# Routing tokens in groups of 10, 10, 5, 5, 3, 2 and 1 tiles, with rank products over shifted columns and one epsilon addition per tile

## The chip, the core and the metric

The kernel runs on one core of one Trainium2 chip. The metric is the device time of one execution in microseconds (us). A core has a matrix engine (TensorE, PE in the rows, with its weight loads shown apart as PEld), VectorE (DVE), ScalarE (ACT), GpSimd (POOL) and SyncE (SP), which issues most DMAs. Each engine works through its own instructions in the order in which they were written, and waits on semaphores for the others.

## The reference

The program chains three parts: pooled attention, a mixture of experts with one expert per token, and a dense feed-forward part.

```python
k_p = k.reshape(B, H, Sp, 8, D).mean(axis=3)      # B, H, S, D = 8, 8, 576, 64; Sp = 72
v_p = v.reshape(B, H, Sp, 8, D).mean(axis=3)
scores = scale * q @ k_p^T
attn = exp(scores - max);  attn = attn / (attn.sum(-1) + 1e-09);  out = attn @ v_p
x = out.transpose(0, 2, 1, 3).reshape(4608, 512)
logits = x @ w_gate + modality_bias[modality_id]  # 8 experts
e_idx = argmax(logits);  gate_w = softmax(logits)[e_idx]
y[token] = gate_w * (relu(x[token] @ w1[e_idx]) @ w2[e_idx])      # 512 -> 1024 -> 512
h = y @ w_in;  result = (h * clip(h + 3, 0, 6) / 6) @ w_out       # 512 -> 2048 -> 512
```

## The kernel before, in words

**Attention** is the first 190 us or so of the program. The 4608 tokens are 36 tiles of 128. The loop at L567 takes one round per tile, for tiles 0 to 32; tiles 33 to 35 follow it, written out. A round works on three tiles at once, so that each tile's work is spread over several rounds:

- `stage_t` (L302) transposes the five blocks of tile i's exponentials on PE into `tps` (L307, this opens the round) and copies them on ACT to `eT` (L309).
- `stage_e` takes the exponentials of tile i + 2 on ACT (L299, L300).
- `stage_x` (L346) multiplies the heads 4 to 7 of tile i - 1 by `rs`, in four ACT instructions (L349), out of the second half of that tile's `ups`.
- `stage_q` transposes the queries of tile i + 4 on PE (L252) and copies them on ACT (L254).
- In some rounds keys and values of a later batch follow (`prep`, `prep2`): PE products `kvps` (L179) and `pw` (L224), ACT copies `vT` (L197), DVE copies `bd` (L188), POOL products `vb` (L231). Pooling of keys and values is DVE's (L173).
- `stage_s` makes the scores of tile i + 3 on PE (`sps`, L281), then on DVE the maxima `mx` (L283) and the differences `d` (L286 or L289).
- `stage_a` (L319) multiplies `eT` of tile i by `vb` on PE into `ups` (L328), in two halves z = 0 and 1 of four heads each, three matmuls a half (twice that for a tile that spans two batches). Each half has a buffer of its own, `u0` and `u1`, in PSUM. DVE then adds the epsilon to each half's sums (L336, two instructions), takes the reciprocal `rs` (L338) and multiplies the heads 0 to 3 (L341). `xo` hands the second half to the next round's `stage_x`.

**Routing.** `ups` carries the gate logits of each head beside its output, so that a row of `xg` holds what the routing of its token needs. Tiles are routed in the groups of `GROUPS`: six of 5 tiles, then 3, 2 and 1. When the last tile of a group is behind, `route` (L361) writes 11 DVE operations on the whole group (and one exponential on ACT) into the list `fill`; `run_fill` (L356) puts one operation of this list behind each DVE operation of `stage_s` and `stage_a`. The first of them (L381) sums the logits over the heads; `oh` (L387) is the one-hot choice of expert.

When all 11 are written, `route_b` (L399) counts on PE how many tokens in front chose the same expert (`rps`, L406): for tile r of n, r matmuls with `ones` and one with the triangle `tri`, and n for the sum over the group. `route_c` (L411) adds five DVE operations (L425 to L429), the last of which casts the row numbers `ix` (L419), and POOL then scatters a tile's rows to DRAM by an indirect DMA (L435), from round `SC0` = 13 two a round. Behind group `FE` = 4 (tiles 20 to 24) `first_expert` (L695) puts 12 small DVE operations in a second list. In round `XL` = 28 what is left in both lists is issued, the scatters that are due are written, and `first_x` (L854) loads the rows of the first expert (`cxg`, by SP at L858) and its weights (`ws`).

**The experts** start in the tail of attention: POOL multiplies the loaded rows by their gate (L829), PE transposes them (`x0`, L837, into `xps`). The two feed-forward parts fill the rest of the program; the change touches nothing there.

The places to follow are `ups` in `stage_a`, `stage_x`, `run_fill`, and the loop's order of calls: `stage_t`, `stage_e`, `stage_x`, `route`, `stage_q`, `prep`s, `stage_s`, `route_b`, `stage_a`, scatters.

Of the kernel before, what the change touches and what calls it, by code (L numbers as in the profile page):

```python
# [8 lines left out]
F32 = mybir.dt.float32  # L9
F32R = mybir.dt.float32r  # L10
BF16 = mybir.dt.bfloat16
# [3 lines left out]
ALU = mybir.AluOpType  # L15
# [4 lines left out]
P = 128  # L20
B, H, S, D = 8, 8, 576, 64
POOL = 8
# [4 lines left out]
E = 8  # L27
# [5 lines left out]
XE = D + E  # L33
GC = H * XE
XW = GC + 2
UX = XE + 1
# [6 lines left out]
REST = (3, 11, 4, 12, 5, 13, 6, 14, 7, 15)  # L43
ORDER = (0, 4, 1, 5, 3, 2, 6)
KR = (0, 160, 288, 448)
GROUPS = ((0, 5), (5, 5), (10, 5), (15, 5), (20, 5), (25, 5), (30, 3), (33, 2), (35, 1))
SC0 = 13
FE = 4
XL = 28
WU = 10  # L50
WS = (-1, -1, 6, 7)
# [22 lines left out]
def attention(tc, g, moe, ins, xr_d):  # L74
    nc = tc.nc
    q, k, v, mid, w_gate, mbias = ins
    es, es_q, es_kv, es_p = ExitStack(), ExitStack(), ExitStack(), ExitStack()
    pool = lambda n, b, st=es, **kw: st.enter_context(tc.tile_pool(name=n, bufs=b, **kw))
    c1 = pool("ac", 1)
    p2 = pool("ap2", 2)  # L80
    p3 = pool("ap3", 3)
    xp = pool("axp", 4)
    rp = pool("arp", 3)
    qp = pool("aq", 3, es_q)
    kvp = pool("akv", 2, es_kv)
# [1 line left out]
    ps_t = pool("ps_t", 1, es_p, space=PSUM)  # L87
    ps_u = pool("ps_u", 1, es_p, space=PSUM)
    ps_q = pool("ps_q", 1, es_p, space=PSUM)

    tiles = []
    for pr in range(B // 2):
# [2 lines left out]
    NTI = len(tiles)  # L95
# [29 lines left out]
    tri = c1.tile([P, P], BF16, name="tri")  # L125
    nc.gpsimd.memset(tri, 1.0)
    nc.gpsimd.affine_select(tri, tri, pattern=[[1, P]], compare_op=ALU.is_gt, fill=0.0, base=0, channel_multiplier=-1)
    ones = c1.tile([P, P], BF16, name="ones")
    nc.gpsimd.memset(ones, 1.0)
    tok = c1.tile([P, NTI], F32, name="tok")  # L130
    t9 = tok.rearrange("p (r t) -> p r t", t=9)
    for c0, n, b0, cm, p0, p1 in ((0, 4, 0, 4, 0, P), (4, 2, S, 4, 0, P), (7, 2, S + 2, 4, 0, P), (6, 1, 512, 1, 0, 64), (6, 1, S + 512, 1, 64, P)):
# [179 lines left out]
    xg = {}  # L312
# [6 lines left out]
    def stage_a(i):  # L319
        o = ETt.pop(i)  # L320
        if i == NTI - 2:
            u = [ps_s.tile([P, 512], F32, name="ups", tag="s")[:, 0:4 * UX].rearrange("p (j x) -> p j x", x=UX) for z in range(2)]
        else:
            u = [ps_u.tile([P, 4, UX], F32, name="ups", tag=f"u{z}") for z in range(2)]
        for z in range(2):
            for n, (c, j, h) in enumerate(((2 * z, 4 * z, 0), (2 * z + 1, 4 * z + 2, 2), (4, 8 + 2 * z, 1))):
                for b, p0, p1 in halves(i):
                    nc.tensor.matmul(u[z][p0:p1, h:h + 2].rearrange("p j x -> p (j x)"), o[:, c, p0:p1],  # L328
                                     vb[b % 3][:, j:j + 2].rearrange("p j x -> p (j x)"), start=n == 0, stop=n == 2)
        j, r, n = group_of(i)  # L330
        if r == 0:
            xg[j] = xp.tile([P, n, XW], F32, name="xg", tag="xg")
        x = xg[j][:, r, 0:GC].rearrange("p (h x) -> p h x", x=XE)
        rs = p3.tile([P, H], F32, name="rs", tag="rs")
        for z in range(2):
            nc.vector.tensor_scalar(rs[:, 4 * z:4 * z + 4], u[z][:, :, XE], POOL * 1e-9, None, op0=ALU.add)  # L336
            run_fill()
        nc.vector.reciprocal(rs, rs)  # L338
        run_fill()
        xo.append((x, u[1], rs))  # L340
        nc.vector.tensor_tensor(x[:, 0:4], u[0][:, :, 0:XE], rs[:, 0:4].unsqueeze(2).to_broadcast([P, 4, XE]), op=ALU.mult)  # L341
        run_fill()
# [8 lines left out]
    fill, fill2 = [], []  # L351
# [4 lines left out]
    def run_fill():  # L356
        for _ in range(rate[0]):
            if fill or fill2:
                (fill or fill2).pop(0)()

    def route(j):  # L361
        i0, n = GROUPS[j]
        x = xg[j]
        sh = [P, n, E]
        v = nc.vector
        t = lambda nm, s_, dt=F32: rp.tile(s_, dt, name=nm, tag=nm)
        l, ex, w, oh = t("l", sh), t("ex", sh), t("w", sh), t("oh", sh, BF16)
        m, m2 = t("m", [P, n, 1]), t("m2", [P, n, 1])

        gs = t("gs", [P, n, 1])  # L370

        def shift():
            v.tensor_tensor(l, l, m.to_broadcast(sh), op=ALU.subtract)
            nc.scalar.activation(ex, l, AF.Exp)

        def last():
            v.reciprocal(x[:, :, GC:GC + 1], gs)
            rt[j] = (x, oh)

        crit = [  # L380
            lambda: v.tensor_reduce(l, x[:, :, 0:GC].rearrange("p n (h x) -> p n x h", x=XE)[:, :, D:XE], AX.X, ALU.add),  # L381
            lambda: v.tensor_tensor(l, l, bia[:, i0:i0 + n], op=ALU.add),
            lambda: v.tensor_reduce(m, l, AX.X, ALU.max),
            shift,
            lambda: v.scalar_tensor_tensor(w, l, 0.0, rev8.unsqueeze(1).to_broadcast(sh), op0=ALU.is_equal, op1=ALU.mult),
            lambda: v.tensor_reduce(m2, w, AX.X, ALU.max),
            lambda: v.tensor_tensor(oh, w, m2.to_broadcast(sh), op=ALU.is_equal),  # L387
        ]
        rest = [
            lambda: v.tensor_copy(x[:, :, GC + 1], tok[:, i0:i0 + n]),  # L390
            lambda: v.tensor_reduce(gs, ex, AX.X, ALU.add),
            lambda: v.tensor_scalar(gs, gs, 1e-9, None, op0=ALU.add),
            last,
        ]
        if j >= len(GROUPS) - 3:
            return crit[:5] + rest[:1] + crit[5:6] + rest[1:2] + crit[6:] + rest[2:]
        return crit + rest

    def route_b(new=lambda: ps_s.tile([P, 512], F32, name="rps", tag="s")):  # L399
        ops = []  # L400
        for j, (x, oh) in list(rt.items()):
            i0, n = GROUPS[j]
            ps = new()
            for r in range(n + 1):
                for r2 in range(min(r + 1, n)):
                    nc.tensor.matmul(ps[:, r * E:(r + 1) * E], tri if r2 == r else ones, oh[:, r2], start=(r2 == 0),  # L406
                                     stop=(r2 == min(r, n - 1)))
            ops += route_c(j, ps, *rt.pop(j))
        return ops

    def route_c(j, ps, x, oh):  # L411
        i0, n = GROUPS[j]
        sh = [P, n, E]
# [95 lines left out]
    ps = kv_ps()  # L509
# [57 lines left out]
    for i in range(NTI - 3):  # L567
        if i == 25:
            es_kv.close()
            moe.open1()  # L570
        if i == NTI - 4:
            es_q.close()
            moe.open2()
        if i == XL:
            each(fill)
            each(fill2)
            del fill[:], fill2[:]
            put_rows()
            tc.add_to_no_dep_group("scatter", moe.first_x())
        stage_t(i)  # L580
        stage_e(i + 2)
        if xo:
            stage_x()
        for j, (a, n) in enumerate(GROUPS):
            if a + n == i:
                fill.extend(route(j))
        if i > 0 and i + 4 < NTI:
            stage_q(i + 4)
        for fn_ in sched.get(i, ()):
            fn_()  # L590
        stage_s(i + 3)
        if i == NTI - 4:
            sp(-1)
        for fn_ in sched2.get(i, ()):
            fn_()
        fill.extend(route_b())
        stage_a(i)
        if i == 0:
            prep_k(1)
            stage_q(4)  # L600
        for _ in range(2):
            if pend and i >= SC0:
                scatter(*pend.pop(0))
    i = NTI - 3
# [41 lines left out]
    ps = unit_table(tc, g, moe.ps)  # L646
# [649 lines left out]
```

## Time and profile before

| what | value |
|---|---|
| median of 3 runs | 1426.13 us (1425.29 to 1426.59) |
| the profiled execution's own time | 1420.61 us |
| its span in the trace | 1418.9 us |
| PE busy over the span | 1371.0 us (97%) |
| DVE, ACT, POOL busy | 940.7, 624.1, 156.5 us (66%, 44%, 11%) |
| loop over tiles 0 to 32, first to last `tps` | 25.3 to 187.9 us |

The profiled execution is 5.5 us below the median of the other runs, so a difference that is worked out from the trace is set against 1420.61 us and then carried over to the median. "Busy" leaves out waits; the busy shares are means over stages that differ. The times of the rows count from the start of the span.

### The profile page before, as it was taken

The numbers are of one execution on the slowest core, as the hardware profiler recorded it, in microseconds if no ns is written. First come the engines' busy times: TensorE is split into PE (matmuls) and PEld (weight loads), VectorE is DVE, ScalarE is ACT, GpSimd is POOL, SyncE is SP. The second block draws the span as 40 slices with busy tenths as digits, with TensorE's granted clock in tenths as the row PEclk, the third lists the DMA queues.
The fourth block names the chain that finished last, engine by engine and source line by source line (L and its number), as shares of the span: only waits on it lengthen the run. The fifth ranks groups of instructions, "written<-read, shape, count | busy, mean of one in ns | idle before, by whom it ended". The sixth has DMA issues, their size and how long they took to land.

```text
span 1418.9 us, 24229 instructions
## 1 busy us (share of the span) xinstructions
PE 1371.0 (97%) x7685; PEld 1263.2 (89%) x7685; DVE 940.7 (66%) x1922; ACT 624.1 (44%) x1262; POOL 156.5 (11%) x190
## 2 busy tenths in 40 slices
PE   7898999999999999999999999999999999999997
PEld 5787889899999999898888888888889888888886
DVE  6988884888888886777787445645654564455443
ACT  3666663555555554444444333423432342244222
POOL 3232341111111111100000100100010010001001
PEclk8999999999999999999999999999999999999999
DMA  9996265777778776665654544553454355445431
GB/s 247 305 299 190 91 198 161 237 242 242 240 243 248 241 242 199 198 210 179 202 162 119 183 137 123 157 165 114 122 181 141 113 150 176 119 116 166 115 116 67
DMA packets 229238, 253.87 MB, mean 179 GB/s; under 512 B 19225, under 2 KB 191293, under 8 KB 229149
## 3 DMA queue, kind: packets, MB, share of 16 engines
q1 hardware_dynamic: 223388, 232.64, 54.7%
q0 software_dynamic: 5760, 20.10, 3.9%
q8 instruction: 50, 0.82, 0.3%
q14 instruction: 40, 0.32, 0.1%
HBM read 206.21 MB, written 46.47 MB: 178 GB/s over the span
## 4 chain that ended last, share of the span: by engine, by line
issue 56%; POOL 2%; DVE 2%; DMA 1%; PE 1%; ACT 0%; SPq 0%; POOLq 0%; DVEq 0%; ACTq 0%
POOL out_dram L1049 2%; DMA ds<-in_moe_w_out_dram 1%; DVE wl L755 1%; DMA ws<-in_moe_w_dram 0%; PE ph L906 0%; DVE lo L911 0%; PE y L919 0%; DVE da L766 0%; DVE dex L777 0%; DVE dm L764 0%; DVE dm L765 0%; DVE dm L768 0%; SPq L820 0%; ACT dex L763 0%; POOLq L1291 0%
## 5 line engine op out<-in xcount | busy, mean ns | idle before, releaser
L1070 PE MATMUL hps<-yc,sq 128*128 128x384 f32 x2004 | 405.1, 337 | 3.3 <-ACT s L1111 1.6
L1070 PEld LDWEIGHTS hps<-yc,sq 128*128 128x128 f32 x2004 | 358.3, 188 | 37.3 <-ACT s L1111 5.5
L1060 PE MATMUL ops<-wo,gh 128*128 128x512 f32 x1152 | 358.5, 392 | 0.0
L1060 PEld LDWEIGHTS ops<-wo,gh 128*128 128x128 f32 x1152 | 211.4, 188 | 23.1
L1060 PE MATMUL ops<-wo,gl 128*128 128x512 f32 x576 | 228.7, 397 | 0.0
L1082 ACT ACTIVATE r<-c,three 128x384 f32<-128x384 f32 x144 | 88.8, 617 | 208.4 <-DVE c L1092 208.0
L755 DVE TENSOR_TENSOR wl<-ws,wh 128x512 fp32r<-128x512 f32 x192 | 132.8, 728 | 35.5 <-ACT wh L754 32.1
L1086 ACT CAST gh<-r 128x384 fp32r<-128x384 f32 x192 | 98.7, 514 | 129.4 <-DVE r L1083 128.0
L754 ACT CAST wh<-ws 128x512 fp32r<-128x512 f32 x192 | 114.5, 619 | 72.2 <-DMA ws<-in_moe_w_dram 54.4
L919 PE MATMUL y<-lo,wh 128*128 128x400 f32 x384 | 133.6, 348 | 1.8 <-DVE lo L911 1.7
L919 PE MATMUL y<-hi,wh 128*128 128x400 f32 x384 | 134.6, 350 | 0.6 <-ACT hi L910 0.5
L906 PE MATMUL ph<-xhi,wh 128*128 128x400 f32 x384 | 132.3, 344 | 2.0 <-PEq L1291 1.2
L906 PE MATMUL ph<-xlo,wh 128*128 128x400 f32 x384 | 132.8, 346 | 0.0
L906 PE MATMUL ph<-xhi,wl 128*128 128x400 f32 x384 | 132.6, 345 | 0.0
L919 PE MATMUL y<-hi,wl 128*128 128x400 f32 x384 | 132.0, 344 | 0.0
L1060 PEld LDWEIGHTS ops<-wo,gl 128*128 128x128 f32 x576 | 107.9, 187 | 23.1
L1087 DVE TENSOR_TENSOR gl<-r,gh 128x384 fp32r<-128x384 f32 x192 | 106.5, 554 | 27.6 <-ACT gh L1086 23.2
L1049 POOL DMA_INDIRECT out_dram<-osb,tki x36 | 35.3, 982 | 777.3 <-ACT osb L1047 745.4
L1083 DVE SCALAR_TENSOR_TENSOR r<-r,c 128x384 f32<-128x384 f32 x144 | 80.4, 558 | 55.1 <-ACT r L1082 53.2
L829 POOL TENSOR_TENSOR cxg<-cxg 100x512 f32<-100x512 f32 x48 | 56.7, 1184 | 348.4 <-PE ph L906 182.6
L1083 DVE SCALAR_TENSOR_TENSOR r<-r,hps 128x384 f32<-128x384 f32 x48 | 26.6, 554 | 97.7 <-ACT r L1082 97.6
L1082 ACT ACTIVATE r<-hps,three 128x384 f32<-128x384 f32 x48 | 27.9, 581 | 131.6 <-PE hps L1070 131.5
(214 smaller groups left out, 1903.6 us busy)
## 6 DMA issues: line engine op xcount, KB each, us to landing
sq<-sd SPq DMA_DIRECT2D x336, 256.0 KB
ws<-in_moe_w_dram SPq DMA_DIRECT2D x192, 256.0 KB, 3.9
sd<-wq SPq DMA_DIRECT2D x16, 896.0 KB
cxg<-xr SPq DMA_DIRECT2D x44, 225.8 KB
yd<-yo SPq DMA_DIRECT2D x12, 800.0 KB
yr<-yd SPq DMA_DIRECT2D x12, 768.0 KB
kv<-in_k_dram SPq DMA_DIRECT2D x16, 512.0 KB
kv<-in_v_dram SPq DMA_DIRECT2D x16, 512.0 KB
```

The costliest lines, as they stand in the source:

```text
L754: nc.scalar.copy(hi, src)
L755: nc.vector.tensor_tensor(lo, src, hi.bitcast(F32), op=ALU.subtract)
L829: nc.gpsimd.tensor_tensor(s.xg[:, t, 0:DM].rearrange("p (h x) -> p h x", x=D), v, s.xg[:, t, GC:GC + 1].unsqueeze(2).to_broadcast([T4, H, ...
L906: nc.tensor.matmul(ph, a[j][:, 0, k * P:(k + 1) * P], b[k], start=(n == 0), stop=(n == 11))
L919: nc.tensor.matmul(yps[d], a[j][:, 1, d * P:(d + 1) * P], b, start=(f == 0 and n == 0), stop=(f == 7 and n == 2))
L1049: i_ = nc.gpsimd.indirect_dma_start(out=out, out_offset=bass.IndirectOffsetOnAxis(ap=tki[:, c:c + 1], axis=0), in_=o, in_offset=None).ins
L1060: nc.tensor.matmul(pso[t_], gt[a][:, t * P:(t + 1) * P], wo[f][:, b], start=(q == 0 and fh == th and n == 0), stop=(q == NQ - 1 and fh != ...
L1070: nc.tensor.matmul(ps, w[:, kk, a * P:(a + 1) * P], y[:, b, kk], start=(start and n == 0), stop=(n == 5), skip_group_check=True)
L1082: a_.activation(r, c, AF.Relu, bias=g.three)
L1083: v.scalar_tensor_tensor(r, r, 6.0, c, op0=ALU.min, op1=ALU.mult)
L1086: a_.copy(gh, r)
L1087: late.append(lambda: v.tensor_tensor(gl, r, gh.bitcast(F32), op=ALU.subtract))
```

## The change

The change does four things.

- `GROUPS` becomes 10, 10, 5, 5, 3, 2 and 1 tiles, and `FE` becomes 2, which again is the group that ends with tile 24. The rows of the groups, which came from a pool of four buffers, stand in one tile `xrows` of 20 rows, at the offsets `ROWS`, used in turn.
- The ranks of a group take n + 1 matmuls instead of about n(n + 3)/2: the one-hots stand side by side in `ohs`, with a zero column block in front of each group, and each matmul with `ones` covers all tiles at one distance d. Over the program that is 43 matmuls instead of 136.
- `ups` is one tile of two PSUM banks, allocated once, in place of the buffers `u0` and `u1`; the epsilon is added by one DVE instruction over both halves (128 x 8), with one operation of `fill` behind it instead of two. Tile 34 keeps the old form.
- In the loop `route` is called behind `stage_s` instead of in front of it, and the exponential of a group's logits is an item of its own in `fill`, one later than before, except in the last three groups.

```diff
-GROUPS = ((0, 5), (5, 5), (10, 5), (15, 5), (20, 5), (25, 5), (30, 3), (33, 2), (35, 1))
+GROUPS = ((0, 10), (10, 10), (20, 5), (25, 5), (30, 3), (33, 2), (35, 1))
+ROWS = (0, 10, 0, 5, 10, 13, 15)
-FE = 4
+FE = 2
...
-    xp = pool("axp", 4)
+    xrows = pool("axp", 1).tile([P, 20, XW], F32, name="xrows")
...
+    ups = ps_u.tile([P, 2, 512], F32, name="ups")
+    u2 = ups[:, :, 0:4 * UX].rearrange("p z (j x) -> p z j x", x=UX)
...
+    ohs = c1.tile([P, NTI + len(GROUPS), E], BF16, name="ohs")
+    nc.gpsimd.memset(ohs, 0.0)
...
         else:
-            u = [ps_u.tile([P, 4, UX], F32, name="ups", tag=f"u{z}") for z in range(2)]
+            u = [u2[:, z] for z in range(2)]
...
         if r == 0:
-            xg[j] = xp.tile([P, n, XW], F32, name="xg", tag="xg")
+            xg[j] = xrows[:, ROWS[j]:ROWS[j] + n]
...
-        for z in range(2):
-            nc.vector.tensor_scalar(rs[:, 4 * z:4 * z + 4], u[z][:, :, XE], POOL * 1e-9, None, op0=ALU.add)
+        if i == NTI - 2:
+            for z in range(2):
+                nc.vector.tensor_scalar(rs[:, 4 * z:4 * z + 4], u[z][:, :, XE], POOL * 1e-9, None, op0=ALU.add)
+                run_fill()
+        else:
+            nc.vector.tensor_scalar(rs.rearrange("p (z j) -> p z j", z=2), u2[:, :, :, XE], POOL * 1e-9, None, op0=ALU.add)
             run_fill()
...
-        l, ex, w, oh = t("l", sh), t("ex", sh), t("w", sh), t("oh", sh, BF16)
+        l, ex, w = t("l", sh), t("ex", sh), t("w", sh)
+        oh = ohs[:, i0 + j:i0 + j + n]
+        late = j < len(GROUPS) - 3
...
-        if j >= len(GROUPS) - 3:
+        if not late:
             return crit[:5] + rest[:1] + crit[5:6] + rest[1:2] + crit[6:] + rest[2:]
-        return crit + rest
+        return crit[:5] + [probs] + crit[5:] + rest
...
-            for r in range(n + 1):
-                for r2 in range(min(r + 1, n)):
-                    nc.tensor.matmul(ps[:, r * E:(r + 1) * E], tri if r2 == r else ones, oh[:, r2], start=(r2 == 0),
-                                     stop=(r2 == min(r, n - 1)))
+            of = ohs[:, i0 + j:i0 + j + n + 1].rearrange("p n e -> p (n e)")
+            for d in range(n + 1):
+                nc.tensor.matmul(ps[:, d * E:(n + 1) * E], ones if d else tri, of[:, 0:(n + 1 - d) * E], start=(d == 0), stop=(d == n))
...
             stage_x()
-        for j, (a, n) in enumerate(GROUPS):
-            if a + n == i:
-                fill.extend(route(j))
...
         stage_s(i + 3)
+        for j, (a, n) in enumerate(GROUPS):
+            if a + n == i:
+                fill.extend(route(j))
```

**Where instructions move: PE, the end of round 2.** `sps` are the scores of tile 5, `ups` the six matmuls of tile 2; `DVE_49`, `Activation_49` and `PE_49` are the semaphores of the three engines, and a line number of the changed kernel lies a few lines further on. Before:

```order
L281 MATMUL sps<-bd_134,qT 128x144 x2
L281 MATMUL sps<-bd_134,qT 128x144 [waits DVE_49,PE_49]
L281 MATMUL sps<-bd_134,qT 128x144
L328 MATMUL ups<-vb_130,eT 128x146 [waits DVE_49,Activation_49]
L328 MATMUL ups<-vb_130,eT 128x146 x2
L328 MATMUL ups<-vb_130,eT 128x146 [waits PE_49,Activation_49]
L328 MATMUL ups<-vb_130,eT 128x146 x2
```

With the change:

```order
L286 MATMUL sps<-bd_136,qT 128x144 x2
L286 MATMUL sps<-bd_136,qT 128x144 [waits DVE_49,PE_49]
L286 MATMUL sps<-bd_136,qT 128x144
L333 MATMUL ups<-vb_132,eT 128x146 [waits DVE_49,Activation_49]
L333 MATMUL ups<-vb_132,eT 128x146 x5
```

The fourth matmul, the first of the second half, has no wait of its own any more; all six stand behind the waits of the first.

**DVE, scores of tile 13 and the end of round 10.** `xg` and `xrows` are the rows of a group, `l` its logits. Before:

```order
L283 TENSOR_REDUCE mx<-sps 128x4
L381 TENSOR_REDUCE l<-xg 128x40
L286 TENSOR_TENSOR d<-sps,mx 128x2x2x72
L382 TENSOR_TENSOR l<-l,bia 128x40
L283 TENSOR_REDUCE mx<-sps 128x4
L383 TENSOR_REDUCE m<-l 128x5
L286 TENSOR_TENSOR d<-sps,mx 128x2x2x72
L373 TENSOR_TENSOR l<-l,m 128x40
```

With the change:

```order
L288 TENSOR_REDUCE mx<-sps 128x4
L291 TENSOR_TENSOR d<-sps,mx 128x2x2x72
L178 TENSOR_TENSOR kv<-kv 128x5x256
L345 TENSOR_SCALAR rs<-ups 128x8
L396 TENSOR_REDUCE l<-xrows 128x80
L347 RECIPROCAL rs<-rs 128x8
L397 TENSOR_TENSOR l<-l,bia 128x80
L350 TENSOR_TENSOR xrows<-ups,rs 128x288
L398 TENSOR_REDUCE m<-l 128x10
```

The first operation of a group's routing, twice as wide, stands behind the scores and the epsilon addition of tile 10; before it stood between the maxima and the differences of the scores.

**DVE, the row numbers of tiles 20 to 24.** `ix` are the row numbers that the scatters of these tiles wait for, `unz` and `ust` belong to `first_expert`. Before, in round 27:

```order
L428 TENSOR_REDUCE pf<-base 128x5
L283 TENSOR_REDUCE mx<-sps 128x4
L419 CAST ix<-pf 128x5
L286 TENSOR_TENSOR d<-sps,mx 128x2x2x72
L701 TENSOR_TENSOR unz<-run,ubs 32x8
```

With the change, at the head of round 28, where what is left in the lists is issued:

```order
L441 TENSOR_TENSOR base<-base,ohs 128x40
L442 TENSOR_REDUCE pf<-base 128x5
L433 CAST ix<-pf 128x5
L715 TENSOR_TENSOR unz<-run,ubs 32x8
L716 TENSOR_REDUCE ust<-unz 32x1
```

The cast moves from the scores of round 27 to behind that round's last operations, with all of `first_expert` behind it and the scores of round 28 after that.

## Rows read from the trace of the kernel before

**Rows 1.** The page: busy time, share of the span and instructions of each engine.

```profile
PE 1371.0 (97%) x7685; PEld 1263.2 (89%) x7685; DVE 940.7 (66%) x1922; ACT 624.1 (44%) x1262; POOL 156.5 (11%) x190
```

**Rows 2.** Windows: start:end length, busy (x) of PE, PEld, DVE, ACT, POOL, PEclk, DMA, GB/s.

```profile
171.53:175.45 3.92, 3.73 (x31) 3.51 (x30) 2.71 (x10) 2.69 (x8) 0.33 (x1) 1.00 0.31 117
...
sum 54.67, PE 53.15 PEld 48.63 DVE 42.47 ACT 39.37 POOL 14.96; mean PE 3.80 PEld 3.47 DVE 3.03 ACT 2.81 POOL 1.07
```

**Rows 3.** Timeline of round 29: start, us, engine, line, operation [idle before <- releaser].

```profile
171.53 0.71 PE L307 MATMUL tps<-idn,e 128*128 128x128 f32 x5
...
172.34 0.69 ACT L309 COPY eT<-tps 128x640 f32<-128x640 f32 x1 [1.23 <-PE tps L307]
...
173.50 0.91 PE L328 MATMUL ups<-vb,eT 128*128 128x146 f32 x6
...
173.60 0.95 ACT L349 ACTIVATE xg<-ups,rs 128x72 f32<-128x72 f32 x4
...
174.60 1.01 PE L328 MATMUL ups<-vb,eT 128*128 128x146 f32 x6 [0.19 <-ACT xg L349]
```

**Rows 4.** Waits, 0 to 245 us: us in total, times, longest.

```profile
PEld ups L328 <- ACT xg L349: 4.5, 14, 0.5
```

**Rows 5.** Timeline of round 9, a `prep2` round that ends at 79.69 us.

```profile
78.09 1.76 PE L328 MATMUL ups<-vb,eT 128*128 128x146 f32 x12
```

**Rows 6.** Windows: rounds 8 (`prep`) and 9 (`prep2`).

```profile
69.12:74.71 5.59, 4.50 (x38) 4.04 (x36) 5.08 (x13) 4.69 (x12) 4.79 (x6) 1.00 1.06 360
74.71:79.69 4.98, 4.98 (x42) 4.67 (x43) 4.67 (x13) 2.69 (x8) 2.77 (x2) 1.00 1.05 346
```

**Rows 7.** Windows: rounds 4, 7 and 31.

```profile
48.42:53.49 5.07, 3.70 (x32) 3.51 (x31) 4.86 (x11) 2.80 (x8) 1.05 (x2) 1.00 1.07 313
64.89:69.12 4.23, 3.76 (x32) 3.58 (x31) 4.20 (x15) 2.69 (x8) 0.25 (x1) 1.00 1.08 294
179.37:183.95 4.58, 4.52 (x52) 4.13 (x51) 4.49 (x23) 2.81 (x9) 0.77 (x1) 1.00 1.00 221
```

**Rows 8.** Windows: rounds 6, 11, 12, 16, 21, 26, with ranks or routing of five tiles.

```profile
59.08:64.89 5.81, 5.67 (x73) 5.08 (x73) 5.78 (x22) 3.01 (x9) 0.00 (x0) 1.00 1.05 310
83.55:89.04 5.49, 4.22 (x51) 4.00 (x50) 5.49 (x23) 2.92 (x9) 0.00 (x0) 1.00 1.12 253
89.04:95.14 6.10, 4.85 (x46) 4.03 (x44) 5.97 (x18) 4.82 (x12) 2.53 (x3) 1.00 0.84 253
107.94:113.89 5.95, 4.29 (x52) 4.07 (x50) 5.92 (x23) 2.92 (x9) 1.61 (x2) 1.00 0.49 146
132.24:139.67 7.43, 5.31 (x66) 4.52 (x64) 7.33 (x25) 5.05 (x13) 1.61 (x2) 1.00 0.12 45
156.44:162.69 6.25, 5.09 (x57) 4.61 (x55) 5.41 (x25) 4.81 (x13) 0.00 (x0) 1.00 0.00 0
```

**Rows 9.** Timeline, 55 to 75 us: the rank products of round 6, and what follows them.

```profile
62.66 0.10 PEld L406 LDWEIGHTS <-tri 128*128 128x128 bf16 x1 [0.30 <-DVE d L286]
...
63.25 1.72 PE L328 MATMUL ups<-vb,eT 128*64 128x146 f32 x24
```

**Rows 10.** Lines by form, DVE, 0 to 245 us: xcount, busy us, mean ns, idle before.

```profile
L336 DVE TENSOR_SCALAR rs<-ups 128x4 f32<-128x4 f32 x72 | 9.5, 154 | 2.3 <-PE ups L328 2.2
...
L381 DVE TENSOR_REDUCE l<-xg 128x40 f32<-128x320 f32 x6 | 4.4, 734 | 3.8 <-ACT xg L349 3.8
```

**Rows 11.** Timeline, 150 to 215 us: the way to the first expert's rows.

```profile
164.80 0.16 DVE L419 CAST ix<-pf 128x5 int32<-128x5 f32 x1
...
174.76 0.37 SPq L858 DMA_DIRECT2D cxg<-xr  x1
...
183.18 4.04 POOL L829 TENSOR_TENSOR cxg<-cxg 100x512 f32<-100x512 f32 x4 [11.32 <-DMA ws<-in_moe_w_dram]
...
188.41 0.51 PE L837 MATMUL xps<-idn,cxg 100*128 100x100 f32 x4
```

**Rows 12.** Windows, 20 to 40 us.

```profile
20.00:40.00 20.00, 16.43 (x107) 15.19 (x108) 16.28 (x41) 10.65 (x27) 3.52 (x4) 0.83 0.88 246
```

More of the change, by code (lines that the diff above doesn't have):

```diff
@@ L373, in shift, with probs @@
             v.tensor_tensor(l, l, m.to_broadcast(sh), op=ALU.subtract)
+            if not late:
+                probs()
+        def probs():
             nc.scalar.activation(ex, l, AF.Exp)
@@ L394, in route @@
         ]
-        if j >= len(GROUPS) - 3:
+        if not late:
             return crit[:5] + rest[:1] + crit[5:6] + rest[1:2] + crit[6:] + rest[2:]
-        return crit + rest
+        return crit[:5] + [probs] + crit[5:] + rest
     def route_b(new=lambda: ps_s.tile([P, 512], F32, name="rps", tag="s")):
```

## The prediction

> **What bounds the kernel now.** I read the page first: PE is busy for 97% of the span [rows 1], so nothing outside PE counts unless PE waits for it. The change touches only attention, so I cut the first 245 us at the rounds' first `tps` and read each round by itself. Fourteen of them (1, 2, 10, 14, 15, 19, 20, 23, 24, 25, 28, 29, 30, 32) are short, with nothing beside tile work: 3.86 to 3.97 us each, 54.67 us in all, and PE is the busiest engine with 3.80 us a round, DVE and ACT at 3.03 and 2.81 [rows 2]. PE is nearly full there, but it is not PE that sets the length. The timeline of round 29 shows the cycle: `tps` opens at 171.53, ACT copies `eT` from 172.34 (after 1.23 us of waiting for `tps`), then the exponentials, then the multiplies of the tile before from 173.60 to 174.55. The first half of `ups` runs beside these multiplies, from 173.50 to 174.41. The second half has to wait 0.19 us for them, starts at 174.60, 3.07 us into the round, and the next `tps` starts 0.85 later, at 175.45 [rows 2, 3]. The weight loads of `ups` name the same wait 14 times [rows 4]. So a short round is one loop: `tps`, `eT`, exponentials, multiplies, half of `ups`, next `tps`. What it depends on is that only half of `ups` stands behind the multiplies.
>
> **The one `ups` tile.** Half 1 of `ups` of tile i overwrites what `stage_x` of tile i - 1 reads; half 0 overwrites what DVE reads (L341). Before, the two halves are two tiles with a wait each. With one tile that is allocated once, the order shows all six matmuls behind the waits of the first. Since `eT` of tile i stands ahead of the multiplies of tile i - 1 in ACT's queue, and the fourth matmul has lost its own wait on ACT, the first one's wait on ACT must be for the multiplies. Then the whole train comes behind them. Run without a break, from its start to the next `tps`, it takes 79.69 - 78.09 = 1.60 us [rows 5, 6]; the x12 of that row are the six matmuls in two passes each, as the x6 of a half are three [rows 3]. A short round becomes 3.02 (end of multiplies) + 0.05 + 1.60 = 4.67 us. Fourteen of them: 65.4 instead of 54.7, **+10.7 us**. Below, the bound is nothing (rival 1), or 0.4 a round if weight loads run ahead of the wait (rival 2); above, 1.01 a round, if a half costs as much as the second half's row is long [rows 3], +14. I take 1.60, from a train that did run without a break.
>
> The `prep` and `prep2` rounds (5.59 and 4.98 us) start `ups` at 3.24 and 3.38, behind 3.07 anyway [rows 5, 6]: no price. Round 4 (5.07, its first half already held by DVE) lies between 0 and +0.9, I take +0.5; round 7 goes from 4.23 to 4.67, round 31 from 4.58 [rows 7]: together **+1.0**.
>
> **Ranks and routing.** The rounds with ranks or routing sum to 37.03 us [rows 8]: DVE is busy for 5.78 of 5.81, 5.49 of 5.49, 5.92 of 5.95 us, so that the one-hot waits in DVE's queue, PE for the ranks, and the `ups` train for PE. With two groups of 10 the routing of tiles 0 to 4 and 10 to 14 disappears as such, and ranks fall away in rounds 6 and 16. In round 6 twenty matmuls take 63.25 - 62.66 = 0.59 us [rows 9]: 5.81 becomes 5.2. Round 16 has nothing left and falls to the new floor, 4.67. Round 11 keeps the first reduce, twice as wide, but behind the scores: between one and two times 0.73 us [rows 10], of which 0.4 shows above the floor: 5.1. Round 12 is a `prep` round and falls towards 5.59: 5.7 with the wide operations in it. Round 21 falls towards the same, 5.7, since the ranks leave it. Round 26 keeps the route of five, without its ranks: 5.6. Sum 31.97, **-5.1 us**; between -5.7, if the wide operations hide wholly, and -3.0, if each costs its full width in DVE's queue.
>
> The ranks go to rounds 12, 22, 27 and 32, where those of 12 stand ahead of a PE that waits for `vT`, so they cost nothing. In 22 and 27, eleven and six matmuls come on top: 0.59/20 = 0.03 us each is the lower bound; the upper one takes them twice as long, as they are up to ten times as wide. I take 0.4 and 0.25, **+0.6 us**.
>
> **What costs or gives nothing.** 35 epsilon additions of 154 ns leave DVE [rows 10], 5.4 us of work, and two groups of 16 small operations with them. In short rounds DVE has 3.03 of 3.9 us to do, and 3.03 of 4.67 afterwards: the ACT chain and PE cover it. If that cover were gone it would be worth up to 0.15 a `prep` round, where DVE is busy 5.08 of 5.59 [rows 6], so -1 us in all, a bound and not in the sum. The memset of `ohs` is POOL's, before the first round, off the path. The later exponential is needed only by `gs`, five operations on.
>
> **The first expert's rows.** The cast of tiles 20 to 24 moves from 164.80, 2.11 us into round 27, to the head of round 28, at least 167.67 by the old clock: some 3.7 us with what stands ahead. On SP the load `cxg` (174.76) stands behind POOL's scatters, on POOL the gate (183.18 to 187.22) behind that, on PE `x0` at 188.41 [rows 11]: 1.19 us to spare. Rounds 28 to 32 get 3.1 us longer by the terms above, so x0 comes later as well and 4.3 covers 3.7. I take 0.3 for it, and 0.5 (0 to 1) for the `ups` of tile 33, which waits for the multiplies of tile 32: **+0.8**. If the rounds did not get longer, x0 would stall by 2.5.
>
> **Sum**: 10.7 + 1.0 - 5.1 + 0.6 + 0.8 = +8.0 us on the profiled 1420.6: 1428.6. That execution lies 5.5 below the median, so the forecast is **1434.1 us**. With its bounds the main case reaches from 1431 (lower route rounds, cheaper train) to 1438.
>
> **Rivals.**
>
> *1. The wait has no price, and the kernel is faster.* Half 0 of `ups` and the multiplies touch different halves; round 29 shows PE write the one from 173.50 to 174.41 while ACT reads the other from 173.60 to 174.55 [rows 3]. If the first matmul's wait is already met, or is for `eT` alone, short rounds stay at 3.9, floors of the route rounds lie 0.75 lower, and these give 0.6 + 0.35 + 1.6 + 0.5 + 2.0 + 1.8 + 0.65 = 7.5 (round 7 with 0.35). Less 0.6 for the moved ranks and 2.5 for x0 that leaves -4.4: 1421.7 us. It decides if `ups` opens before 3.02 in short rounds. Against it: the lost wait of the fourth matmul. The Trainium skill, PSUM — Partial Sum Buffer, Terms, has collisions of two engines only within one bank and quadrant, so the hardware itself would let the two banks of the new tile be written and read at once; round 29's overlap agrees. By that rule the wait would be left out and the time would be rival 1's. But a wait is what the program holds, and the order shows it moved. Chance 0.11.
>
> *2. The price is half.* If the loads of `eT` weights run ahead of the wait, and the tail of the train goes beside the next round's start, a short round costs 0.4 more (5.6 in all), and with -5.7 in the route rounds, +1.0, +0.6 and +0.8 the sum is +2.3: 1428.4 us, within measurement of no change. Against it: `PEld` itself has the wait, not the matmul alone [rows 4]. Chance 0.11.
>
> *3. The clock falls.* PE would have a gap of about 0.75 us in each short round. In the stretch from 20 to 40 us, with PE busy for 16.43 us, the granted clock was 0.83 in the mean [rows 12], so partly the lower level of 1.2 GHz. Were one such stretch added, 20 x 0.17 / 0.5 = 6.8 us at the low level would hold 3.4 us of work more: 1437.5 us and above. For it: the new gaps, round after round; against it: round 4, with 3.70 us busy of 5.07, at a granted clock of 1.00, 2.4 GHz [rows 7]. Chance 0.05.
>
> **How the numbers follow.** The main case has 0.73. About 0.2% (2.85 us) is what a measurement can tell from no change. Faster holds rival 1, 0.11, and a corner of rival 2: 0.12; same is the rest of rival 2 and the main case's lowest end: 0.13; slower is what is left, 0.75. The range has to hold 8 in 10: the main case, rival 2's upper half and rival 3: 1427 to 1440; rival 1 is left out.
>
> **What would show it.** Right: short rounds of 4.6 to 4.7 us with the first `ups` matmul 0.05 behind the last multiply and six in one train, the wait for the multiplies named in over 14 rounds, route rounds 6 and 16 shorter by 0.6 and 1.3, and loop end about 7 us later. Wrong: `ups` opening at 2 us in short rounds (rival 1); short rounds near 4.3 (rival 2); a granted clock under 1.00 after 40 us (rival 3); or x0 waiting for `cxg` by more than 1 us.

## The result and the profile after

The changed kernel takes 1439.97 us (median of 5 runs, 1438.48 to 1441.77), the kernel before 1425.29 us in the same series of runs (1422.77 to 1426.59): a ratio of 1.0104, 95% interval [1.0091, 1.0118], so about 14.7 us slower. The direction was forecast; the forecast of 1434.1 us was 8.0 us over 1426.13, so some 45% of the loss was not in it. The changed kernel's profiled execution took 1438.48 us.

In some series of runs TensorE's signals come late while GpSimd scatters, whatever the kernel: the trace of before that the prediction was worked out from (1420.61 us) had none of this, and the changed kernel's trace has it.

The page, first row, to be held against [rows 1]: PE, DVE, ACT and POOL are busy for nearly as long as before; the span is 17.8 us longer and PE's share falls by 2 points. The added time is waiting.

```profile
PE 1369.3 (95%) x7592; PEld 1263.8 (88%) x7592; DVE 939.3 (65%) x1855; ACT 624.3 (43%) x1260; POOL 154.4 (11%) x191
```

The timeline of an undisturbed short round of the changed kernel (round 28), which answers to [rows 3]:

```profile
181.45 0.71 PE L312 MATMUL tps<-idn,e 128*128 128x128 f32 x5
...
183.46 0.94 ACT L358 ACTIVATE xrows<-ups,rs 128x72 f32<-128x72 f32 x4
...
184.46 1.76 PE L333 MATMUL ups<-vb,eT 128*128 128x146 f32 x12 [0.88 <-ACT xrows L358]
```

`ups` is one train of six matmuls (x12 passes), 0.06 us behind the end of the multiplies, and PE has been idle for 0.88 us. Before, the first half ran beside the multiplies. The windows of the short rounds, as in [rows 2]: three of the fourteen, and their sum.

```profile
159.50:170.61 11.11, 5.27 (x31) 5.04 (x30) 2.51 (x8) 2.68 (x8) 6.83 (x8) 0.70 0.45 173
181.45:186.05 4.60, 3.72 (x31) 3.50 (x30) 3.99 (x23) 2.68 (x8) 1.81 (x2) 1.00 0.15 56
186.05:191.34 5.29, 3.73 (x31) 3.51 (x30) 1.71 (x6) 2.68 (x8) 2.99 (x4) 1.00 0.60 233
...
sum 72.81, PE 53.70 PEld 50.15 DVE 50.67 ACT 39.71 POOL 29.13; mean PE 3.84 PEld 3.58 DVE 3.62 ACT 2.84 POOL 2.08
```

Ten of the fourteen last 4.60 to 4.71 us. Round 25 lasts 11.11 us, more than twice as long as any in [rows 2]: PE is busy for 5.27 us of it, DVE and ACT for 2.5 and 2.7, and the granted clock is 0.70. The rounds of [rows 8]:

```profile
59.64:64.66 5.02, 5.02 (x53) 4.51 (x54) 4.71 (x12) 2.68 (x8) 0.00 (x0) 1.00 1.01 274
84.79:90.06 5.27, 3.72 (x31) 3.51 (x30) 5.01 (x15) 2.96 (x9) 0.00 (x0) 1.00 0.16 49
90.06:96.00 5.94, 5.15 (x57) 4.33 (x55) 5.81 (x16) 4.80 (x12) 1.61 (x2) 1.00 0.62 212
110.29:118.72 8.43, 4.99 (x32) 4.76 (x31) 3.00 (x8) 2.69 (x8) 4.28 (x5) 0.85 0.98 320
139.01:144.90 5.89, 4.84 (x45) 4.02 (x43) 5.60 (x16) 4.82 (x13) 1.61 (x2) 1.00 0.02 4
170.61:176.32 5.71, 4.62 (x36) 4.17 (x34) 4.58 (x18) 4.71 (x13) 0.00 (x0) 0.98 0.00 0
```

Round 16 (the fourth) went up from 5.95 to 8.43 us although its routing and ranks are gone. The waits, 0 to 245 us, against [rows 4]: the wait for the multiplies has grown from 4.5 to 28.9 us (the longest, 6.1, is in round 25), and a releaser appears that the trace of before does not have in attention, "remote", a signal for which the trace shows no instruction that had just ended.

```profile
PEld ups L333 <- ACT xrows L358: 28.9, 18, 6.1
...
ACT eT L314 <- remote: 7.0, 1, 7.0
DVE rs L345 <- remote: 5.7, 1, 5.7
```

The timeline of round 25 shows what stands behind it.

```profile
159.50 0.76 PE L312 MATMUL tps<-idn,e 128*128 128x128 f32 x5
160.11 0.60 PE L257 MATMUL qps<-idn,q 128*128 128x128 f32 x4
160.15 0.96 POOL L449 DMA_INDIRECT xr<-xrows,ix  x1 [0.30 <-issue]
160.54 1.15 PE L286 MATMUL sps<-bd,qT 128*128 128x144 f32 x8
161.41 0.96 POOL L449 DMA_INDIRECT xr<-xrows,ix  x1 [0.30 <-issue]
162.67 0.96 POOL L449 DMA_INDIRECT xr<-xrows,ix  x1 [0.30 <-issue]
...
165.22 0.17 DVE L345 TENSOR_SCALAR rs<-ups 128x8 f32<-128x8 f32 x1 [5.67 <-remote]
165.27 0.69 ACT L314 COPY eT<-tps 128x640 f32<-128x640 f32 x1 [6.99 <-remote]
```

PE's records put `tps` at 159.50 to 160.26. ACT waits for nothing but them, and starts 5 us later; DVE, which waits for the `ups` in front of them, starts at the same moment. The trace also keeps the moment at which a semaphore rises. PE's rose at 163.64 and then six times from 165.08 to 165.37, 0.04 to 0.07 us apart; in the trace of before one rises within 0.05 us of a matmul's end. The packets of the run of eight scatters that begins at 153.68 run from 155.3 to 165.1 us. So by the records PE's signals, not its work, were held, and were let go together as the last of these packets ended. (The ends of matmuls in the records are modelled, so they cannot show by themselves that the results were there.) The signals of ACT and DVE that the trace keeps come within 0.02 us of the end of their instruction. The same happens in round 16, from 107 us on, in the run of ten scatters that begins at 99.70.

### The profile page after: what moved, and what is told of

Read it like the earlier page. It is cut to its first block, busy times and chain, and to the rows that moved or that the text cites. A ratio compares the mean times of both kernels' runs of the same rounds, so it can differ in the third digit from the quotient of the medians.

```text
span 1436.7 us, 23958 instructions
## 1 busy us (share of the span) xinstructions
PE 1369.3 (95%) x7592; PEld 1263.8 (88%) x7592; DVE 939.3 (65%) x1855; ACT 624.3 (43%) x1260; POOL 154.4 (11%) x191
## 4 chain that ended last, share of the span: by engine, by line
issue 55%; POOL 2%; PE 2%; DVE 1%; DMA 1%; ACT 0%; POOLq 0%; SPq 0%; DVEq 0%; ACTq 0%
POOL out_dram L1063 2%; PE ph L920 1%; PE y L933 1%; DVE wl L769 1%; DMA ws<-in_moe_w_dram 0%; DMA ds<-in_moe_w_out_dram 0%; DVE lo L925 0%; DVE dm L782 0%; DVE da L780 0%; DVE dex L791 0%; ACT dex L777 0%; POOLq L1305 0%; ACT wh L768 0%; DVE xlo L769 0%; DVE dm L778 0%
## 5 line engine op out<-in xcount | busy, mean ns | idle before, releaser
L333 PE MATMUL ups<-vb,eT 128*128 128x146 f32 (+1 forms) x480 | 65.9, 302 | 30.5 <-ACT xrows L358 24.0
```

## The experiments

Each kernel was compared with the kernel before in its own series. That kernel took 1418.41 us in the first series (e1 to e4), 1426.16 in the second (e5 to e8), 1426.71 in the third (e9 to e12), 1418.35 in the fourth (e13 to e16) and 1424.69 in the fifth (e17, e18). No profile of the first and fourth series has a late signal of PE; every one of the others has 16 to 42 that rise more than 0.12 us behind the matmul's record. The first three series ran on a chip of one and the same number, so the chip alone does not decide it.

### First series: which part costs

e1 undoes the merged tile and its one epsilon addition, e2 makes these two alone, e3 undoes the groups of ten, e4 undoes both.

```diff
 # e1, e4 (the epsilon additions left out here)
...
-            u = [u2[:, z] for z in range(2)]
+            u = [ps_u.tile([P, 4, UX], F32, name="ups", tag=f"u{z}") for z in range(2)]
 # e3, e4 (ROWS and FE left out here)
...
+GROUPS = ((0, 5), (5, 5), (10, 5), (15, 5), (20, 5), (25, 5), (30, 3), (33, 2), (35, 1))
```

> The changed kernel with ups in two one-bank tiles and two epsilon additions again; groups of ten, n + 1 ranks and the order of the loop stay. Theory A (the merged tile puts the whole ups train behind the multiplies): short rounds go back from 4.61-4.71 to 3.86-3.97 us, 10 us less. Theory B (the late TensorE signals in rounds 16, 25 and 29 come from runs of up to ten scatters): they stay, rounds 16 and 25 are still 7 to 10 us long, and the time is about 5 us over the kernel before. Theory C (the late signals need the merged tile, whose waits leave TensorE idle in every short round): they are gone as well, and the time is 4 to 6 us under the kernel before.

> The kernel before with the merged ups tile and the single epsilon addition alone; groups of five and the old ranks stay. A: short rounds 4.6 to 4.7 us, 10 to 12 us over the kernel before. B: no late TensorE signals, since no run has more than five scatters: 10 to 12 us in all. C: late signals as in the changed kernel, 3 to 6 us in each run of scatters that meets short rounds: 16 to 22 us over the kernel before.

> The changed kernel with the groups of before (six of 5, then 3, 2, 1); the merged tile, n + 1 ranks and the order of the loop stay. A: short rounds still 4.6 to 4.7 us. B: no late signals, the time is 6 to 9 us over the kernel before. C: late signals stay, 12 to 18 us over.

> The changed kernel with the groups of before and ups in two tiles: what is left of the change is the n + 1 ranks, the order of the loop and the row buffer. A: short rounds 3.9 us; no late signals under B or C. Ranks save 0.5 us in each round that has them behind VectorE, and the first reduce no longer stands between the scores: 2 to 5 us under the kernel before.

Measured: e1 1419.54 us, ratio 1.0004 [0.9994, 1.0014]; e2 1429.22 us, 1.0075 [1.0057, 1.0093]; e3 1429.12 us, 1.0081 [1.0061, 1.0101]; e4 1419.30 us, 0.9995 [0.9982, 1.0009]. The two kernels with the merged tile lose 11 us, the two without it nothing: theory A holds, with its size. For e2, the wait for the multiplies (against [rows 4]), and in windows the sums of the fourteen short rounds and of the six of [rows 8]:

```profile
PEld ups L330 <- ACT xg L355: 18.5, 17, 1.6
...
sum 65.09, PE 52.09 PEld 48.47 DVE 47.59 ACT 39.42 POOL 14.84; mean PE 3.72 PEld 3.46 DVE 3.40 ACT 2.82 POOL 1.06
...
sum 33.78, PE 29.58 PEld 26.40 DVE 31.37 ACT 23.65 POOL 5.36; mean PE 4.93 PEld 4.40 DVE 5.23 ACT 3.94 POOL 0.89
```

The merged tile takes the short rounds from 54.67 to 65.09 us. B and C were not decided: late signals were missing in all four. e1 did not win the 4 to 6 us that were expected without them, though its rounds got shorter; the sums of the same two groups of rounds in e1:

```profile
sum 54.68, PE 53.20 PEld 48.79 DVE 45.91 ACT 38.59 POOL 20.32; mean PE 3.80 PEld 3.49 DVE 3.28 ACT 2.76 POOL 1.45
...
sum 32.96, PE 27.15 PEld 24.05 DVE 31.75 ACT 23.01 POOL 11.19; mean PE 4.53 PEld 4.01 DVE 5.29 ACT 3.84 POOL 1.86
```

The six rounds of [rows 8] give back 4.1 us. In its trace the tail takes it back: POOL's gate ends at 185.78, and PE's transposes of the first expert's rows (`xps`) wait for it part by part.

```profile
180.85 4.93 POOL L837 TENSOR_TENSOR cxg<-cxg 100x512 f32<-100x512 f32 x4 [10.69 <-DMA cxg<-xr]
...
182.94 0.31 PE L845 MATMUL xps<-idn,cxg 100*128 100x100 f32 x1 [0.63 <-POOL cxg L837]
184.38 0.31 PE L845 MATMUL xps<-idn,cxg 100*128 100x100 f32 x1 [1.14 <-POOL cxg L837]
185.83 0.31 PE L845 MATMUL xps<-idn,cxg 100*128 100x100 f32 x1 [1.14 <-POOL cxg L837]
```

Round 33 takes 4.55 us there against 1.55 before, and in the next one, behind these gaps, the granted clock is 0.60, partly the level of 1.2 GHz; that round takes 4.30 us instead of 3.37. The late row numbers, priced at 2.5 us if the rounds did not get longer, cost 3.0 there when they don't, and 0.9 more by the clock. e4, which was to be 2 to 5 us under the kernel before, shows the same: its loop is 4.6 us shorter than in the first trace, and rounds 33 and 34 take 4.94 and 5.04 us.

### Second series: is it the kernel, and can the tail be mended

e5 is the changed kernel again. e6 is e4, e8 is e1, both with earlier row numbers; e7 halves the scatters of a round.

```diff
 # e6, e8
     for i in range(NTI - 3):
+        rate[0] = 2 if 25 <= i < XL else 1
 # e7
-        for _ in range(2):
+        for _ in range(1):
             if pend and i >= SC0:
```

> The changed kernel once more, unaltered. If the late TensorE signals belong to the kernel (theories B and C joined: merged tile and groups of ten together, since neither alone had them), rounds 16 and 25 are again 8 to 11 us long and the time is 13 to 17 us over the kernel before. If they were an accident of one execution, rounds 16 and 25 are 4.7 us and the time is 8 to 11 us over, as with the merged tile alone.

> As e4 (groups of five, two ups tiles, n + 1 ranks, the new order of the loop), but two operations of the list behind each VectorE operation in rounds 25 to 27, so that the row numbers of tiles 20 to 24 come at the end of round 26 instead of round 27. Theory D (what the shorter loop wins is lost because the transposes of the first expert's rows wait for the chain row numbers, scatters, load, gate, and the low clock after that): round 33 is back at 1.6 us, the clock stays at 2.4 GHz there, and the time is 4 to 6 us under the kernel before. Rival E (TensorE work of the tail and the experts' weights set the end anyway): the wait goes, but the time stays within 2 us of the kernel before.

> The changed kernel with one scatter a round in GpSimd's program in place of two, so that values for the next batch stand between them and no run before round 28 has more than about five scatters. If the late signals come from a run of scatters longer than five, rounds 16 and 25 are 4.7 us here. If they come from any scatters beside a merged tile in groups of ten, they stay. From round 28 on nine scatters stand in one run, and the first expert's rows come some 5 us later.

> As e1 (groups of ten, two ups tiles) with the same early row numbers as e6. D: round 33 back at 1.6 us, 4 to 6 us under the kernel before. E: within 2 us of it.

Measured: e5 1443.68 us, ratio 1.0114 [1.009, 1.0138]; e6 1428.09 us, 1.0007 [0.9994, 1.0021]; e8 1435.66 us, 1.0065 [1.0045, 1.0085]; e7 1441.26 us (one run). e5 repeats rounds 16 and 25 (9.02 and 11.23 us), so they were no accident. But e6 and e8, whose relatives e4 and e1 had no late signal, have them as well: neither B nor C can be the whole story. In e6 round 33 is back at 1.55 us, as D says, and the gain does not show, since five rounds with runs of five scatters (10, 15, 20, 25, 28) take 31.42 us instead of the 19.6 of e4. e7 did not do what it was made for: the trace still shows ten scatters in a row from 99.11 us: nothing in the program holds GpSimd to the round, and it takes the next scatter. It is inconclusive.

### Third series: the same kernels again, and the kernel before

No edits: e9 is the kernel before, e10 is e1, e11 is e2, e12 the changed kernel.

> The kernel before, unaltered, with a profile of its own. Late TensorE signals were in every profile of one series of runs (e5 to e8, groups of five with two tiles among them) and in none of another (e1 to e4). Theory F: they belong to a condition of the chip that holds for a series, and strike any kernel in its runs of scatters. Then in a series that has them, this kernel has five rounds (about 12, 17, 22, 27 or 28) 1.5 to 3 us longer than in its first profile, and 1424 to 1428 us; in a series without, 1416 to 1421 us. Theory G: they need a part of the change (the row buffer or the order of the loop, common to e5 to e8); then this kernel never shows them.

> e1 once more (groups of ten, two tiles). F: in a series with late signals, rounds 15, 16, 25 and 26 are 10 to 15 us longer together than in e1, and the time is 5 to 9 us over the kernel before; in a series without, as e1, within 2 us of it.

> e2 once more (the kernel before with the merged tile alone). Without late signals 9 to 12 us over the kernel before. With them: short rounds of 4.6 us leave room, so that part of the lateness hides; 8 to 12 us over.

> The changed kernel a third time. F: in a series without late signals the loop has only the price of the merged tile and the gains of the routing: rounds 16 and 25 are 4.7 us, and the time is 8 to 11 us over the kernel before; in a series with them 14 to 17 us over.

Measured: e9 1427.05 us, ratio 1.0006 [0.9995, 1.0016]; e10 1433.54 us, 1.0045 [1.0025, 1.0064]; e11 1437.57 us, 1.0081 [1.0058, 1.0104]; e12 1442.72 us, 1.0118 [1.0093, 1.0143]. F holds: the kernel before has late signals too. Its rounds 14, 24, 28 and 29 in windows, against 3.86, 3.97, 3.86 and 3.92 us in the first trace:

```profile
98.49:103.15 4.66, 4.00 (x31) 3.56 (x30) 4.35 (x11) 2.69 (x8) 1.09 (x1) 1.00 1.07 353
...
148.38:153.52 5.14, 4.00 (x44) 3.34 (x42) 4.90 (x12) 2.68 (x8) 0.59 (x1) 1.00 0.26 104
...
168.72:173.49 4.77, 4.00 (x32) 3.56 (x31) 1.75 (x11) 2.80 (x8) 3.27 (x4) 1.00 0.58 220
173.49:178.53 5.04, 3.93 (x32) 3.56 (x30) 4.12 (x13) 2.78 (x8) 0.00 (x0) 1.00 0.27 84
```

With round 19 (4.58 us against 3.86) they cost it 4.7 us from round 8 to 32. F had named other rounds, and 1.5 to 3 us for each. e10 and e1 are one kernel, but with late signals it is 6.8 us over the kernel before, without them 1.1. Its windows for rounds 15, 16 and 25:

```profile
104.27:109.53 5.26, 3.99 (x43) 3.30 (x41) 3.78 (x10) 2.69 (x8) 4.13 (x4) 1.00 1.04 410
109.53:117.81 8.28, 4.92 (x31) 4.45 (x30) 3.90 (x12) 2.69 (x8) 3.97 (x5) 0.91 0.97 327
...
156.62:166.73 10.11, 5.20 (x31) 4.62 (x30) 4.37 (x12) 2.68 (x8) 7.98 (x9) 0.87 0.50 193
```

They stood at 3.97, 3.98 and 3.97 us in e1. The merged tile alone (e11) costs 10.9 us here and 10.8 in the first series: within the intervals that price is the same in both.

### Fourth and fifth series: length or place of the scatters

e13 is the kernel before with the n + 1 products alone (the edits to `route_b` and `ohs` of the change). e14 routes the first groups one round later. e15 is e1, e16 is e6, with a copy in front of a round's scatters that waits for DVE's `rs` of that round.

```diff
 # e14
-            if a + n == i:
+            if a + n + (j < FE) == i:
 # e15, e16 (the tile pace left out here)
+        if pend and i >= SC0:
+            nc.gpsimd.tensor_copy(pace, xo[-1][2][:, 0:1])
```

> The kernel before with the n + 1 rank products alone; groups of five, two tiles, and the order of the loop stay, so that the scatters start where they did. The rank train of five tiles falls from 0.59 us to about 0.2, the rest of those rounds is VectorE's: 1 to 3 us less in the loop, and 0 to 3 us under the kernel before with or without late signals, since no run of scatters moves.

> The kernel before with the first four groups routed one round later, so that their runs of five scatters lie in short rounds instead of the long rounds with keys and values. Theory H (place): in a series with late signals each of the runs at rounds 14 to 15 and 19 to 20 costs 1.5 to 3 us instead of 0.8, and the time is 3 to 8 us over the kernel before. Theory I (length): runs of five are too short to matter wherever they lie, and the time is within 2 us of it.

> e1 (groups of ten, two tiles) with a small GpSimd copy of the round's rs in front of each round's scatters, so that GpSimd really issues two a round instead of ten in a row. Theory I (length): lateness grows within a run from some 4 to 6 us after its start, so that pairs never get there: rounds 15, 16, 25 and 26 are as in e1, and the time is within 3 us of the kernel before in any series. H (place): the scatters lie in short rounds still, and 5 us or more remain.

> e6 (groups of five, two tiles, n + 1 ranks, early row numbers) with the same pacing. I: no late signals in rounds 10, 15, 20 and 25, round 33 at 1.6 us, and the time is 3 to 7 us under the kernel before. H: as e6, within 2 us of it.

Measured: e13 1417.71 us, ratio 0.9996 [0.9986, 1.0006]; e14 1414.74 us, 0.9972 [0.9959, 0.9986]; e15 1419.65 us, 1.0015 [1.0005, 1.0024]; e16 1416.52 us, 0.9999 [0.9988, 1.0009]. The series had no late signals, so H and I could not be told apart. The ranks alone are worth nothing that can be measured; the loop of e13, which was to be 1 to 3 us shorter, is 1.4 longer than in the first trace, with 7.23 us and a granted clock of 0.81 in round 16. e16, which is e6 with the copy and here without late signals, decides between D and E: round 33 is at 1.55 us and the loop 3.9 us shorter than in the first trace, but the time is the same within 1.7 us, as E says, and not 3 to 7 us lower. So the tail explains the lost gain in the trace of e1, but mending it won nothing that the runs show, and why is open. e14 is faster than the kernel before, without being meant to be: rounds 11, 16 and 21 fall to 3.91, 3.97 and 5.59 us. So e14 and e15 ran once more.

> e14 once more. Without late signals 3 to 5 us under the kernel before, as in e14. With them: H (place) 0 to 6 us over it, since the runs of five now lie in short rounds; I (length) 2 to 5 us under it.

> e15 once more (groups of ten, two tiles, two scatters a round). Without late signals within 3 us of the kernel before. With them: I (length) within 3 us of it, and rounds 15, 16, 25, 26 as in e1; H (place) 5 us or more over it, as e10.

Measured, now with late signals: e17 1425.87 us, ratio 1.0007 [0.9993, 1.002]; e18 1428.28 us, 1.0021 [1.0005, 1.0036]. Five kernels ran unaltered in a series without late signals and in one with them. The table has the growth of rounds 8 to 32 from one trace to the other, and that of the median time:

| kernel | runs of scatters | without | with | price, trace | price, medians |
|---|---|---|---|---|---|
| before (first trace, e9; first and third series) | five | 118.75 | 123.44 | 4.7 us | 8.3 us |
| merged tile alone (e2, e11; first and third) | five | 124.73 | 131.06 | 6.3 us | 8.4 us |
| ten, two tiles (e1, e10; first and third) | ten; eight, two | 115.26 | 129.85 | 14.6 us | 14.0 us |
| one round later (e14, e17; fourth and fifth) | five | 115.02 | 121.35 | 6.3 us | 11.1 us |
| ten, held (e15, e18; fourth and fifth) | four, five, one; four, four, two | 115.24 | 124.40 | 9.2 us | 8.6 us |

The kernel before pays 6.3 us by its medians of the fourth and fifth series, so the pairs of series are not equally severe. The copy did not make pairs of the scatters, as it was meant to: by e18's trace the runs are broken only into pieces of up to five. In the traces the price is 5.4 us lower for it, with round 25 at 5.66 instead of 10.11 us, though round 26 goes from 5.97 to 7.69. Rounds 16, 25 and 26 of e18:

```profile
106.73:113.67 6.94, 4.75 (x31) 4.31 (x30) 2.75 (x9) 2.69 (x8) 6.14 (x8) 0.90 0.97 295
...
152.49:158.15 5.66, 4.05 (x31) 3.61 (x30) 1.82 (x6) 2.69 (x8) 4.56 (x7) 1.00 0.61 239
158.15:165.84 7.69, 4.77 (x38) 4.10 (x36) 6.28 (x23) 5.02 (x13) 3.92 (x6) 1.00 0.29 115
```

By the traces, moving runs of five into short rounds adds only 1.6 us (e17). But that profiled execution (1421.67 us) was the fastest of its ten runs, 4.2 us under their median. By medians, over what the kernel before pays in the same two series, runs of five in short rounds cost 4.8 us, runs of ten 5.7, and the broken ones 2.3. So both length and place count, and which weighs more is not decided. Neither H nor I holds alone: e17 lies 1.0 us over the kernel before, which is in the range of H, while theory I had it 2 us or more under; e18 lies 3.0 us over it, less than the 5 of H, but its round 16 takes 6.94 us, which by theory I was to stay at 3.98. e6, with runs of five, grew by 12.8 us over e4, from which it differs by the early row numbers too. What decides it within a round stays open.

## Why the prediction was right in direction and short in size

- **The one `ups` tile: right.** Forecast 4.67 us a short round and 65.4 in all; the change has 4.60 to 4.71 where nothing disturbs, and e2 a sum of 65.09. Rounds 4 and 7 were undersized (+0.9 and +0.7 for +0.5 and +0.4). Rival 1, the wait without a price, and rival 2, half of it, are out: the 10.8 us of e2 decide it, and the wait that the program holds goes by the tile. The Trainium skill, PSUM — Partial Sum Buffer, Terms, speaks of collisions within one bank and quadrant, which the two banks of the tile would not be. By that alone rival 1 would have held.
- **Ranks and routing: right in the rounds, with one exception.** Forecast 5.2, 5.1, 5.7, 5.7 and 5.6 us for rounds 6, 11, 12, 21 and 26; measured 5.02, 5.27, 5.94, 5.89 and 5.71. Round 16 was to be 4.67 and took 8.43. The ranks moved to rounds 22 and 27 cost 0.30 and 0.14, not 0.4 and 0.25.
- **The first expert's rows: right.** In the changed kernel the gate ends before the transposes want it, and round 33 is 1.55 us, as before:

```profile
200.99 4.03 POOL L843 TENSOR_TENSOR cxg<-cxg 100x512 f32<-100x512 f32 x4 [11.04 <-DMA ws<-in_moe_w_dram]
...
206.60 0.51 PE L851 MATMUL xps<-idn,cxg 100*128 100x100 f32 x4
```

The longer rounds are that cover, and e1, without them, stalls just there.
- **The step that failed is in the sum:** "That execution lies 5.5 below the median, so the forecast is 1434.1 us." The gap was carried over as a constant. By all that the runs show, most of it was a mechanism: e9 has 4.7 us of late signals in the kernel before, which the first trace did not have, and 1426.13 us is the level of the series with them (1424.7 to 1426.7, against 1418.4 without); the three runs behind that median were not traced. With runs of scatters twice as long the price grows. The part on routing, too, gave the groups of ten no price for their scatters: that term stood at nothing, and the scatters were followed only as far as the expert's rows. In the changed kernel's trace this is 3.8 us in round 16, 6.4 in round 25, and some 1.8 in rounds 17, 29, 30 and 32: 12.0 us, against 12.4 by which the loop grew beyond the forecast (19.6 for 7.2). Between the medians less is left of it, since the kernel before pays too.
- **Rival 3, the clock,** came in part. In the changed kernel's own trace it is a consequence: 0.85 and 0.70 in rounds 16 and 25, behind the gaps that the late signals made, while the gaps of 0.88 us in ordinary short rounds left it at 1.00. But round 4, which the prediction held against this rival, is where it came by itself. With the whole train behind the multiplies PE waits 2.23 us there. In four of the seven traces with the merged tile (e3, e5, e11, e12) the granted clock of that round is 0.78 to 0.83, partly the level of 1.2 GHz, and the round takes 7.12 to 7.41 us instead of 5.93; in the thirteen traces with two tiles it stays at 1.00 and takes 5.07 to 5.09 us. Round 4 in the changed kernel's first trace and in e12, the same kernel:

```profile
48.12:54.05 5.93, 3.70 (x31) 3.51 (x30) 5.76 (x11) 2.79 (x8) 1.04 (x2) 1.00 1.16 246
...
48.66:55.78 7.12, 4.89 (x32) 4.69 (x31) 6.07 (x11) 2.80 (x8) 1.83 (x3) 0.83 1.13 270
```

By parts, with late signals: 10.9 us for the merged tile (e11) and 6.8 for all the rest (e10), 17.7 together, where the change itself measured 14.7, 17.5 and 16.0 us. What it would cost without them was not measured. There e2 and e1 add up to 12 us, of which 3.9 are the tail of e1 that the longer rounds of the change cover; an estimate from these runs is therefore some 8 to 12 us.

## What to carry to other kernels

Two buffers merged into one save an instruction and lose a degree of freedom: before merging, read in the order which waits of the second half move to the first instruction, and price them in the round whose loop runs through them. A gap between the profiled execution and the median of the runs is itself a finding: before it is carried over as a constant, look for what could fill it, and ask whether the change multiplies it. And work that is off the path (scatters) can hold back the signals on the path, so the length and the place of such runs belong into the sum.

## What the runs showed of the hardware that was not expected

While GpSimd issues scatters some 1.3 us apart, TensorE's semaphore signals can be held. The first late one comes 2 to 8 us after a run of scatters begins, the last at most 1.9 us after the run's last scatter; in the longest case seen, round 25 of the changed kernel, one was held by about 5 us, and then six came within 0.3 us. The signals of ScalarE and VectorE that these traces keep come within 0.02 us of the end of their instruction. It happens in whole series of runs (three of the five here, beside the changed kernel's own) and not at all in others, for the same program and on a chip of the same number, and is worth 6 to 8 us to the kernel before (1418.4 against 1424.7 to 1426.7 us). What sets it off was not found: the scatters' packets take as long with it as without (a median of 187 ns for a packet of 4624 bytes in the first trace and in the changed kernel's). The trace's PE records hide it, since they go on as if nothing were held; it shows as "remote" releasers and as ACT and DVE starting together long after PE's record has ended.

The same wait was followed by a lower granted clock in some executions of a program and not in others: round 4 of the changed kernel, with PE idle for 2.23 us, ran at 1.00 in one of its three traces (5.93 us) and at 0.80 and 0.83 in the other two (e5 and e12, 7.38 and 7.12 us).
